# A hand-written order reworked: roots in two parts, decoding moved out of attention, eight first-layer units in a row, the last routing ahead of its weights

## The chip, the core and the metric

The kernel runs on one core of a Trainium2 chip. The metric is the device time of one execution in microseconds (us). The core has a matrix engine (TensorE, PE), a vector engine (VectorE, DVE), a scalar engine (ScalarE, ACT) and a general one (GpSimd, POOL), which take their instructions in the order of the program and wait for each other by semaphores; transfers are issued by SP's queue, and indirect ones (gather, scatter) by POOL.

## The reference

Three layers follow one another: attention with normalised queries and keys, a mixture with one expert (a leaky two-layer network whose weights come in 64-bit floats), and a mixture of eight experts in which each token goes to the one with the largest logit. Shapes: 4 batches, 12 heads, 448 rows, 64 columns a head; 1792 tokens of 768; 2048 columns in the first network, 1024 in each expert of the second.

```python
q_n, k_n = (rmsnorm(q, g_q), rmsnorm(k, g_k))        # x / sqrt(mean(x*x) + 1e-6) * g
scores = scale * np.matmul(q_n, k_n.transpose(0, 1, 3, 2))
scores = scores - np.max(scores, axis=-1, keepdims=True)
attn = np.exp(scores)
attn = attn / (np.sum(attn, axis=-1, keepdims=True) + 1e-09)
x = np.matmul(attn, v)                                # -> (1792, 768)

h = x @ w_in
x = np.maximum(0.01 * h, h) @ w_out                   # first MoE

logits = x @ w_gate
e_idx = np.argmax(logits, axis=1)
gate_w = probs[np.arange(N), e_idx]                   # softmax of the logits
eom = 1.0 / (1.0 + np.exp(-(x @ w_output_gate)))
for e in range(E):                                    # second MoE
    h = np.maximum(x[mask] @ w1[e], 0.0)
    out[mask] = gate_w[mask, None] * eom[mask, e, None] * (h @ w2[e])
```

## The kernel before

**Arithmetic.** Nearly every product is made of three matmuls: each operand is split into a high part (a copy on ACT) and a low part (the difference, `lo_of`, line 62, on DVE or POOL), and high by high, high by low and low by high are added in PSUM.

**Attention** works on 24 pairs of heads, two heads at a time on 128 partitions. Of each pair: `square`, `roots` and `norm` (DVE, POOL) normalise; `turn_q`/`turn_k` transpose; `top` makes the scores of one chunk of 112 rows and takes their row maxima into `md` (DVE); `row` transposes the four `md` on PE and copies them into `mx` (ACT, L296), which `probs` needs; `values` multiplies by V, and adds the probabilities into `pr` on POOL; `sums`, `spread`, `scale` and `store` divide by the sums and write the columns. While pair i has its `probs`, the tops of i+1 and the normalising of later pairs run beside it. A hand-written list says which step goes into which of the four quarters: `begin` (line 466) for pairs 0 to 2, `steady` for the others from `FROM` = 3, and `pieces` (line 380) for what stands ahead and behind.

**The first MoE** reads weights as pairs of 32-bit words. `Weights.half` (line 616) decodes half a tile in five steps, `magnitude`, `sign`, `flush`, `power` and `join`, with one DVE instruction each and, beside them, one on ACT and, at the end, an addition on POOL; `split` (line 651) makes the high half on ACT and the low half on POOL. There are 64 halves. Six of them (and one that starts them) are decoded within attention, at the pairs in `DECODE`. A unit m1 (`FirstMoe.first`, line 667) is one of 16 columns blocks f for one batch b: 18 matmuls into a `mo` bank (there are two), then `out`: g on ACT, the maximum on DVE, `gh` on ACT, `gl` on DVE. A unit m2 (`second`, line 690) is one of six output blocks d: 6 matmuls into an `mp` bank, of two f, added into `ysum`. Two f are a group G; there are eight groups, and a tile is a group for one batch. In group 0 the units are set in order by hand; from group 1 on each tile does the new m1 units, then the m2 units of the tile before, and `tile` (line 957) says which unit is followed by which steps of two halves.

**Routing** (`Route`, line 716) runs per batch: `logits` of six blocks, `read_logits` (`lt`), `turn_logits`, `pick` (the expert), `rank` and `place` (the slot of each token), `table` (matmuls of `A`, `Bm` that put token numbers and weights into `tab` and `stab`). `column` writes a block of the first MoE's output, turned, to `x2d` in DRAM through buffers `xn`. The last route runs behind the last m2 units. From `tab` follows `idx`, the list of tokens for each of 18 slot tiles.

**The second MoE** takes slot tile after slot tile: `gather` (POOL, indirect), `prep` (transposes, and `xgh`, `xgl`), `m1` into `ph`, `relu`, `turn`, `m2` into `py`, and a scatter. Expert weights come in the stretch before, as `w1h`, `w1l`, `w2h`, `w2l`. The order of PE, DVE, ACT and POOL is written by hand (`tc.manual_schedule`) up to the last route's choice, and again from the first gather.

## Time and profile before

| what | us |
| --- | --- |
| median of three runs | 1193.51 (1193.49, 1193.51, 1194.4) |
| the profiled execution | 1190.01 |
| its span in the trace | 1188.3 |
| PE busy in it | 1130.5 (95%) |
| mean granted clock | 0.981 |

The profile has one line an engine with its busy time, and lists of instructions with their start, their duration and, in brackets, how long the engine was idle before them and who ended that. PE being busy 95% says that it bounds the kernel, but this is a mean over stages: what can be won is read stage by stage, as idle time of PE and as stretches in which its clock is at the lower of its two levels.

### The profile page before, as it was taken

The page shows a single profiled execution, that of the slowest core. Times are in us where ns is not written, and L with a number is a line of the kernel's source. Part 1 is how long each engine was busy: PE and PEld are TensorE (multiplying, and loading weights), DVE is VectorE, ACT ScalarE, POOL GpSimd, SP SyncE. Part 2 cuts the span into 40 slices and gives each one's busy share as a digit, 9 for nine tenths or more (in the row PEclk, how much of TensorE's full clock was granted, in tenths as well). Part 3 has the DMA queues.
Part 4 walks back from the last instruction along what each step waited for, and adds up shares of the span by engine and source line. Part 5 has one row for each costly group of instructions (what it writes and reads, how often), then busy time and mean ns, then how long its engine had stood idle before and what let it go on. Part 6 is the DMA issues. An engine that isn't in the chain of part 4 may idle for free.

```text
span 1188.3 us, 18150 instructions
## 1 busy us (share of the span) xinstructions
PE 1130.5 (95%) x6620; PEld 912.5 (77%) x6620; DVE 809.8 (68%) x1384; ACT 496.4 (42%) x791; POOL 391.3 (33%) x267
## 2 busy tenths in 40 slices
PE   5899999998999999999999999998699999999997
PEld 3455555444689889998989898886599998998996
DVE  8787888988656888888888887354644179115445
ACT  4566666655444222222222222213443277225444
POOL 3767677777423322222222222000102113102022
PEclk9999999989999999999999999999699999999999
DMA  7222222111111211111111111523555169214446
GB/s 144 60 63 66 60 63 69 40 33 51 40 54 50 59 52 55 53 55 53 54 53 54 54 54 41 200 49 96 171 207 210 40 240 372 113 36 161 165 189 234
DMA packets 68075, 116.21 MB, mean 98 GB/s; under 512 B 6780, under 2 KB 45948, under 8 KB 67968
## 3 DMA queue, kind: packets, MB, share of 16 engines
q1 hardware_dynamic: 64848, 103.87, 27.5%
q0 software_dynamic: 3120, 11.02, 2.7%
q8 instruction: 54, 0.88, 0.3%
q14 instruction: 53, 0.43, 0.1%
HBM read 106.61 MB, written 12.58 MB: 100 GB/s over the span
## 4 chain that ended last, share of the span: by engine, by line
PE 76%; DVE 15%; issue 4%; ACT 4%; DMA 1%; POOL 0%; POOLq 0%; ACTq 0%; DVEq 0%
PE mp L697 6%; PE mp L699 6%; PE mp L698 6%; PE mo L674 5%; PE mo L675 5%; PE mo L676 5%; PE sc L310 5%; PE py L1158 4%; PE py L1156 4%; PE py L1157 4%; PE ph L1141 4%; PE av L321 4%; PE ph L1142 4%; PE ph L1140 4%; DVE md L289 3%
## 5 line engine op out<-in xcount | busy, mean ns | idle before, releaser
L326 POOL TENSOR_TENSOR pr<-pr,p 112x896 f32<-112x896 f32 x71 | 150.4, 2119 | 21.9 <-PE av L321 19.8
L645 POOL TENSOR_TENSOR raw<-raw,top 128x384 f32<-128x384 f32 x64 | 66.3, 1036 | 258.9 <-DVE raw L644 258.9
L697 PE MATMUL mp<-gh,w1h 128*128 128x448 f32 x384 | 144.2, 376 | 5.0 <-DVE ysum L705 2.5
L699 PE MATMUL mp<-gh,w1l 128*128 128x448 f32 x384 | 142.1, 370 | 1.2 <-POOL w1l L63 1.2
L674 PE MATMUL mo<-xTh,w0h 128*128 128x448 f32 x384 | 141.5, 369 | 1.0 <-DVE gl L63 1.0
L698 PE MATMUL mp<-gl,w1h 128*128 128x448 f32 x384 | 141.9, 370 | 0.2 <-DVE gl L63 0.2
L675 PE MATMUL mo<-xTl,w0h 128*128 128x448 f32 x384 | 140.8, 367 | 0.0
L676 PE MATMUL mo<-xTh,w0l 128*128 128x448 f32 x384 | 140.0, 365 | 0.0
L1204 POOL DMA_INDIRECT out_dram<-y,idx x18 | 36.1, 2004 | 264.1 <-DVEq L1199 149.6
L705 DVE TENSOR_TENSOR ysum<-mp,ysum 128x448 f32<-128x448 f32 x168 | 100.9, 616 | 18.7 <-PE mp L699 18.7
L289 DVE TENSOR_REDUCE md<-tp 112x2 f32<-112x896 f32 x94 | 101.9, 1084 | 15.7 <-PE tp L287 15.3
L63 DVE TENSOR_TENSOR hL<-pt,hT 128x512 fp32r<-128x512 f32 x36 | 24.9, 692 | 114.1 <-ACTq L1166 59.4
L1156 PE MATMUL py<-w2h,hT 128*128 128x384 f32 x288 | 99.8, 346 | 0.0
L1158 PE MATMUL py<-w2l,hT 128*128 128x384 f32 x288 | 96.8, 336 | 0.0
L1157 PE MATMUL py<-w2h,hL 128*128 128x384 f32 x288 | 96.6, 335 | 0.0
L682 ACT ACTIVATE g<-mo 128x448 f32<-128x448 f32 x64 | 34.8, 544 | 135.3 <-PE mo L676 135.3
L312 ACT ACTIVATE p<-sc 112x896 f32<-112x896 f32 x72 | 65.7, 912 | 55.5 <-PE sc L310 52.6
L1140 PE MATMUL ph<-w1h,xgh 128*128 128x512 f32 x216 | 86.1, 398 | 0.0
L1142 PE MATMUL ph<-w1l,xgh 128*128 128x512 f32 x216 | 85.1, 394 | 0.0
L1141 PE MATMUL ph<-w1h,xgl 128*128 128x512 f32 x216 | 85.1, 394 | 0.0
L697 PEld LDWEIGHTS mp<-gh,w1h 128*128 128x128 f32 x384 | 72.6, 189 | 14.9 <-DVE ysum L705 5.2
L699 PEld LDWEIGHTS mp<-gh,w1l 128*128 128x128 f32 x384 | 72.9, 190 | 8.4 <-POOL w1l L63 1.6
(207 smaller groups left out, 2444.8 us busy)
## 6 DMA issues: line engine op xcount, KB each, us to landing
r<-in_moe_w_dram SPq DMA_DIRECT2D x27, 1024.0 KB, 5.3
r<-in_moe_w_dram SPq DMA_DIRECT2D x36, 768.0 KB, 7.8
wd<-in_moe_w_in_dram SPq DMA_DIRECT2D x32, 384.0 KB, 3.4
wd<-in_moe_w_out_dram SPq DMA_DIRECT2D x32, 384.0 KB, 3.1
qk<-in_q_dram SPq DMA_DIRECT2D x24, 224.0 KB, 3.0
qk<-in_k_dram SPq DMA_DIRECT2D x24, 224.0 KB, 3.3
vv<-in_v_dram SPq DMA_DIRECT2D x24, 224.0 KB, 2.6
x2d<-xn SPq DMA_DIRECT2D x24, 224.0 KB, 3.0
```

Of the source, the lines that this page charges most:

```text
L289: nc.vector.tensor_reduce(st["md"][:, c, ::DH], sc[:CP, :, :S], AX.X, ALU.max)
L326: nc.gpsimd.tensor_tensor(st["pr"][:CP], st["pr"][:CP], p, ALU.add)
L674: nc.tensor.matmul(ph, wh_[:, c], xh, start=(c == 0), stop=False)
L675: nc.tensor.matmul(ph, wh_[:, c], xl, start=False, stop=False)
L676: nc.tensor.matmul(ph, wl_[:, c], xh, start=False, stop=(c == KD - 1))
L697: nc.tensor.matmul(py, hi[:, sl], gh, start=(j == 0), stop=False)
L698: nc.tensor.matmul(py, hi[:, sl], gl, start=False, stop=False)
L699: nc.tensor.matmul(py, lo[:, sl], gh, start=False, stop=(j == GF - 1))
L1140: nc.tensor.matmul(ph[n], xh[:, c], w1h[:, c, s_], start=(c == 0), stop=False)
L1156: nc.tensor.matmul(py[n], hT[:, c], w2h[:, c, s_], start=(c == 0), stop=False)
L1157: nc.tensor.matmul(py[n], hL[:, c], w2h[:, c, s_], start=False, stop=False)
L1158: nc.tensor.matmul(py[n], hT[:, c], w2l[:, c, s_], start=False, stop=(c == K2 - 1))
```

## The change

1. **Start.** `roots` can be done in two parts, of four and five instructions. `begin` has a new list: the pairs' roots from pair 1 on are done in the two parts a and b, `row` and `spread` stand behind `values`, `store` behind the turns. The first pair's four tops stand in a row, and `route_constants` comes ahead of the loop instead of in pair 12.
2. **Decoding.** `DECODE` has 21 and 22 only (it had 15, 17, 19, 20, 21, 22), so that four halves fewer are decoded within attention. The first `split` moves from the first to the last quarter of pair 22, and the one in the last section leaves it; the two fills are block f = 0 for batches 0 and 1. The order of weights goes by group: both input blocks, both output blocks.
3. **Group 0.** Eight m1 units stand in a row, with the halves h3 to h7 and their splits between them, then 24 m2 units with eight halves. The steady tiles get one step of decoding behind every six matmuls.
4. **Routing.** A table's matmuls stand a slot behind the `A`, `Bm` that they need, `Bm` is made on POOL, columns go in pairs. In the last route all six logit groups come first, the logits are read ahead of the columns, `xn` has buffers of its own, and no `w1l` stands in between. The weights (`weigh`, `stab`, `rsc`) move into slot tile 0, between the last `ph` and the first `py`. The first gather stands alone; `w1l` 1, 3, 5 are on DVE, and 0, 2, 4 on POOL behind that gather.

```diff
-        def roots(self, sts):
+        def roots(self, sts, parts=(0, 1)):
...
-            todo = ({0: ["s2"], 1: ["g2", "n2"], 2: ["q3"], 3: ["s3"]},
-                    {0: ["q4"], 1: ["s4"], 2: ["g3", "n3"], 3: ["q5"]},
-                    {0: ["s5", "q6"], 1: ["s6"], 2: ["g5", "q7"], 3: []})[i]
+            todo = ({0: ["s2"], 1: ["g2", "n2"], 2: ["q3"], 3: ["q4", "s3"]},
+                    {0: ["s4"], 1: ["a3"], 2: ["b3", "q5"], 3: ["q6", "s5"]},
+                    {0: ["s6"], 1: ["a5"], 2: ["b5", "q7"], 3: []})[i]
+            after = ({}, {2: (3,)}, {0: (4,), 2: (5,)})[i]
...
                     else:
-                        self.norm(sts[k], (1, 0))
-                if c == 3:
-                    self.row(one)
-                    if prev:
-                        self.spread(prev)
+                        self.roots(sts[k:k + 2], ("ab".index(op[0]),))
                 if c:
                     self.values(cur, c - 1)
...
                 elif c == 3:
+                    self.row(one)
                     if prev:
+                        self.spread(prev)
                         self.scale(prev)
...
-    DECODE = 15, 17, 19, 20, 21, 22
+    DECODE = 21, 22
...
-            self.order = [(kind, f) for kind in range(2) for f in range(GF)]
-            self.order += [(kind, f) for f in range(GF, NF) for kind in range(2)]
+            self.order = [(kind, f) for G in range(NG) for kind in range(2) for f in range(G * GF, (G + 1) * GF)]
...
-        if i == B * NPAIR - 2 and q == 0:
+        if i == B * NPAIR - 2 and q == 3:
             wts.split()
...
+    h4, h5, h6, h7 = (wts.half() for _ in range(4))
+    plan = [[wts.split, *h4[:1]], h4[1:3], h4[3:], h5[:2], h5[2:3], h5[3:], [wts.split, *h6[:1]]]
+    plan += [[x] for x in h6[1:4]] + [[h6[4], h7[0]], h7[1:2], h7[2:3], h7[3:], [wts.split]]
+    done = len(plan)
+    do([("m1", 0, 0, 2), ("m1", 0, 0, 3)] + [("m1", 0, 1, b) for b in range(B)], plan)
...
+            plan = [[x] for x in halves(0, 1)]
+            if b in (1, 3):
+                at(plan, 11, wts.split)
...
-    for d, unit in enumerate(group("m2", NG - 1, B - 1)):
-        steps = list(extra[d])
-        if d:
-            steps += [lambda d=d: late.logits(d - 1), lambda d=d: late.column(d - 1)]
-        moe.run(unit, steps)
-    late.logits(KD - 1)
-    late.column(KD - 1)
+    own = wts.pools[0]
+    for d in range(KD):
+        late.logits(d)
+    late.read_logits()
+    late.columns((0, 1), own)
+    late.turn_logits()
+    late.pick()
...
+        if t == 0:
+            weights_made()
         for c in range(4):
             m2(0, c)
...
+    def low1(c):
+        lo_of(nc.vector if c % 2 else nc.gpsimd, w1l[:, c], r1[c // 2][:, c % 2], w1h[:, c])
+
+    def weights_made():
+        n = NC * P
+        room = sb.tile([P, D], F32, name="y2")
+        late.weigh()
+        late.weigh_more()
+        pt = p2.tile([P, 3, P], F32, name="pt")[:, 0]
+        for c in range(NC):
+            Bm, A = room[:CP, c * P:(c + 1) * P], room[:CP, n + c % 2 * NTAB:n + (c % 2 + 1) * NTAB]
+            nc.gpsimd.tensor_scalar(Bm, place, late.pf[:, c:c + 1], None, ALU.is_equal)
+            nc.vector.tensor_scalar(
+                A, iota[:CP, :NTAB], late.col[:, c:c + 1], late.z[:, c:c + 1], ALU.is_equal, ALU.mult)
+            nc.tensor.matmul(pt[:NTAB], A, Bm, start=(c == 0), stop=(c == NC - 1))
+        nc.vector.tensor_tensor(stab, pt[:NTAB], stab, ALU.add)
+        pt = p2.tile([P, 3, P], F32, name="pt")[:, 0, :NSLOT]
+        nc.tensor.matmul(pt, stab, perm, start=True, stop=True)
+        nc.vector.tensor_copy(rsc, pt)
```

The first place is POOL's queue in the last section of attention, with the kernel before; `raw` is the addition that ends a half, `w0l` a split's low part, `pr` the sums of probabilities.

```order
L645 TENSOR_TENSOR raw<-raw,top 128x384
L326 TENSOR_TENSOR pr_126<-pr_126,p 112x896 x2
L63 TENSOR_TENSOR w0l<-raw,w0h 128x768
L326 TENSOR_TENSOR pr_124<-pr_124,p 112x896
L645 TENSOR_TENSOR raw<-raw,top 128x384
L326 TENSOR_TENSOR pr_124<-pr_124,p 112x896 x2
L63 TENSOR_TENSOR w0l<-raw,w0h 128x768
```

The same stretch of POOL after the change (its line numbers are those of the changed kernel).

```order
L645 TENSOR_TENSOR raw<-raw,top 128x384
L330 TENSOR_TENSOR pr_126<-pr_126,p 112x896 x2
L330 TENSOR_TENSOR pr_124<-pr_124,p 112x896
L645 TENSOR_TENSOR raw<-raw,top 128x384
L330 TENSOR_TENSOR pr_124<-pr_124,p 112x896
L63 TENSOR_TENSOR w0l<-raw,w0h 128x768
L330 TENSOR_TENSOR pr_124<-pr_124,p 112x896
L330 TENSOR_TENSOR pr_126<-pr_126,p 112x896 x2
```

The first `w0l` now stands behind a further `raw` and two more additions into `pr`.

The second place is DVE in group 0, with the kernel before; L683 is the maximum of a unit m1, `gl` its low part, L631 to L644 are the five steps of a half.

```order
L683 TENSOR_TENSOR mo<-mo,g 128x448
L63 TENSOR_TENSOR gl<-mo,gh 128x448
L683 TENSOR_TENSOR mo<-mo,g 128x448
L63 TENSOR_TENSOR gl<-mo,gh 128x448
L631 TENSOR_SCALAR top<-wd 128x384
L634 SCALAR_TENSOR_TENSOR top<-wd,top 128x384
L637 SCALAR_TENSOR_TENSOR top<-raw,top 128x384
L641 TENSOR_SCALAR raw<-top 128x384
L644 SCALAR_TENSOR_TENSOR raw<-wd,raw 128x384
L683 TENSOR_TENSOR mo<-mo,g 128x448
```

DVE in the eight units after the change.

```order
L685 TENSOR_TENSOR mo<-mo,g 128x448
L63 TENSOR_TENSOR gl<-mo,gh 128x448
L629 TENSOR_SCALAR top<-wd 128x384
L632 SCALAR_TENSOR_TENSOR top<-wd,top 128x384
L636 SCALAR_TENSOR_TENSOR top<-raw,top 128x384
L640 TENSOR_SCALAR raw<-top 128x384
L644 SCALAR_TENSOR_TENSOR raw<-wd,raw 128x384
L685 TENSOR_TENSOR mo<-mo,g 128x448
L63 TENSOR_TENSOR gl<-mo,gh 128x448
```

There is now a whole half between one unit and the next, in unit after unit.

The third place is DVE around slot tile 0, with the kernel before; `xgl` is the low part of the gathered rows, `w1l` and `w2l` those of the expert's weights, `hL` that of the hidden layer.

```order
L63 TENSOR_TENSOR xgl_8255<-pt,xgh_8253 128x384 x2
L63 TENSOR_TENSOR w1l<-r_1_7303,w1h 128x1024
L63 TENSOR_TENSOR w1l<-r_2_7304,w1h 128x1024 x2
L63 TENSOR_TENSOR w2l<-r_0_7305,w2h 128x768 x2
L63 TENSOR_TENSOR w2l<-r_1_7306,w2h 128x768 x2
L1125 TENSOR_LOAD flags
L63 TENSOR_TENSOR hL<-pt,hT 128x512
L63 TENSOR_TENSOR w2l<-r_2_7307,w2h 128x768 x2
L63 TENSOR_TENSOR w2l<-r_3_8244,w2h 128x768 x2
L63 TENSOR_TENSOR hL<-pt,hT 128x512
```

DVE there after the change, up to the first of the `w2l`.

```order
L63 TENSOR_TENSOR w1l<-r_0_7310,w1h 128x1024
L63 TENSOR_TENSOR w1l<-r_1_7311,w1h 128x1024
L63 TENSOR_TENSOR w1l<-r_2_7312,w1h 128x1024
L63 TENSOR_TENSOR xgl_8231<-pt,xgh_8229 128x384 x2
L63 TENSOR_TENSOR w2l<-r_0_7313,w2h 128x768 x2
```

And DVE from the first `hL` on; `kz`, `ksm`, L1253, `stab` and `rsc` make the weights.

```order
L63 TENSOR_TENSOR hL<-pt,hT 128x512
L63 TENSOR_TENSOR w2l<-r_2_7315,w2h 128x768 x2
L63 TENSOR_TENSOR w2l<-r_3_8220,w2h 128x768 x2
L835 TENSOR_REDUCE kz<-kz_8196 112x4
L841 TENSOR_REDUCE ksm<-kd_8195 112x4
L842 TENSOR_SCALAR ksm<-ksm 112x4
L843 TENSOR_SCALAR kz<-kz 112x4
L844 TENSOR_TENSOR kz<-kz,ksm 112x4
L845 RECIPROCAL kz<-kz 112x4
L1253 TENSOR_SCALAR y_8371<-iota,kcol,kz 112x112 x4
L1256 TENSOR_TENSOR stab<-pt,stab 112x128
L1259 COPY rsc<-pt 128x21
```

All `w1l` of DVE now stand ahead of `xgl`, and the weights' steps behind the four `w2l`.

## Rows read from the trace of the kernel before

**Rows 1.** Page, engines: busy us (share of the span) x instructions.

```profile
PE 1130.5 (95%) x6620; PEld 912.5 (77%) x6620; DVE 809.8 (68%) x1384; ACT 496.4 (42%) x791; POOL 391.3 (33%) x267
```

**Rows 2.** Windows: A:B us, busy (x instructions), PEclk, DMA share, GB/s.

```profile
73.72:162.63 88.91, 88.91 (x707) 47.58 (x708) 72.79 (x125) 60.04 (x89) 66.42 (x41) 1.00 0.22 63
162.63:276.43 113.80, 105.83 (x795) 54.76 (x796) 100.08 (x171) 67.62 (x102) 80.82 (x49) 0.97 0.17 48
315.80:388.00 72.20, 70.10 (x336) 63.53 (x333) 42.25 (x67) 31.89 (x60) 18.46 (x14) 0.98 0.17 51
388.00:745.00 357.00, 353.65 (x1717) 321.71 (x1718) 292.41 (x481) 94.79 (x170) 96.89 (x74) 1.00 0.18 53
745.00:827.65 82.65, 77.46 (x584) 67.24 (x586) 41.52 (x140) 18.76 (x40) 1.40 (x1) 0.98 0.38 117
827.65:852.46 24.81, 14.62 (x92) 11.40 (x92) 11.72 (x51) 9.68 (x15) 3.21 (x3) 0.62 0.35 94
```

**Rows 3.** Windows, stretches at the lower clock level.

```profile
58.88:62.29 3.41, 3.24 (x12) 1.50 (x12) 1.47 (x3) 1.89 (x5) 3.29 (x3) 0.50 0.45 135
260.26:267.09 6.83, 6.83 (x26) 2.95 (x25) 3.82 (x10) 3.17 (x6) 4.33 (x3) 0.50 0.20 58
331.94:335.36 3.42, 3.33 (x9) 2.99 (x10) 2.90 (x8) 1.30 (x3) 0.03 (x1) 0.50 0.00 0
813.22:816.64 3.42, 3.42 (x14) 3.13 (x13) 2.82 (x11) 0.00 (x0) 0.00 (x0) 0.50 0.02 5
833.70:854.18 20.48, 13.21 (x59) 10.26 (x60) 12.71 (x51) 8.99 (x14) 4.21 (x4) 0.50 0.31 88
```

**Rows 4.** Waits of PE, 0 to 90: total us, times, longest us.

```profile
PE tr L294 <- DVE md L289: 6.3, 4, 3.7
```

**Rows 5.** Timeline, DVE and POOL: start us, us, instruction.

```profile
53.37 2.06 DVE L220 TENSOR_SCALAR y<-ms 112x32 int32<-112x32 int32 x1
...
51.12 4.28 POOL L326 TENSOR_TENSOR pr<-pr,p 112x896 f32<-112x896 f32 x2
```

**Rows 6.** Timeline, POOL's second `w0l`, and PE's first use of one.

```profile
305.49 1.83 POOL L63 TENSOR_TENSOR w0l<-raw,w0h 128x768 fp32r<-128x768 f32 x1
...
304.45 0.36 PE L676 MATMUL mo<-xTh,w0l 128*128 128x448 f32 x1
```

**Rows 7.** Windows, a half decoded alone, and one beside POOL.

```profile
349.88:352.42 2.54, 2.54 (x14) 2.32 (x14) 2.33 (x7) 1.34 (x4) 0.00 (x0) 1.00 0.17 68
364.53:368.63 4.10, 4.10 (x21) 3.76 (x21) 3.89 (x7) 2.83 (x7) 1.85 (x1) 1.00 0.17 59
```

**Rows 8.** Groups of DVE, 388 to 745: busy us, mean ns, idle.

```profile
L63 DVE TENSOR_TENSOR gl<-mo,gh 128x448 fp32r<-128x448 f32 x49 | 30.6, 624 | 29.9 <-ACT gh L684 29.9
L683 DVE TENSOR_TENSOR mo<-mo,g 128x448 f32<-128x448 f32 x48 | 30.0, 626 | 20.9 <-ACT g L682 20.9
```

**Rows 9.** Waits of PE, 745 to 827.65.

```profile
PE mp L697 <- ACT gh L684: 1.8, 1, 1.8
```

**Rows 10.** Timeline, last route to first `ph`: ACT, DVE, POOL, PE.

```profile
834.16 0.26 ACT L748 ACTIVATE lt<-lg 128x112 f32<-128x112 f32 x1
...
835.53 1.22 DVE L63 TENSOR_TENSOR w1l<-r,w1h 128x1024 fp32r<-128x1024 f32 x1
...
846.62 1.21 POOL L1108 DMA_INDIRECT xg<-x2d,idx  x1 [100.22 <-DVE idx L1069]
...
852.46 0.80 PE L1140 MATMUL ph<-w1h,xgh 128*128 128x512 f32 x1
```

**Rows 11.** Timeline, a decoding step of DVE and a POOL split.

```profile
324.36 2.11 DVE L634 SCALAR_TENSOR_TENSOR top<-wd,top 128x384 int32<-128x384 int32 x1
...
324.21 1.84 POOL L63 TENSOR_TENSOR w1l<-raw,w1h 128x768 fp32r<-128x768 f32 x1 [9.65 <-ACT w1h L657]
```

**Rows 12.** Timeline, slot tile 0: DVE, PE.

```profile
860.99 3.55 DVE L63 TENSOR_TENSOR w2l<-r,w2h 128x768 fp32r<-128x768 f32 x4
...
862.14 0.33 PE L1156 MATMUL py<-w2h,hT 128*128 128x384 f32 x1
```

More of the change, by code (lines that the diff above doesn't have):

```diff
@@ L602, in fetch @@
             kind, f = self.order[k]
-            own = self.more if g and self.more else dec
+            own = self.more if self.more and not g else dec
             wd = own.tile([P, n, 2], I32, name="wd", bufs=WD)
@@ L953, in do, with halves @@
     def do(units, plan=()):
-        for u, unit in enumerate(units):
-            moe.run(unit, plan[u] if u < len(plan) else ())
-    def tile(first, second, end):
-        a, b_ = wts.half(), wts.half()
-        return [first + a[:3], a[3:] + b_[:2], [], b_[2:3], b_[3:4], b_[4:], end]
+        slots = [list(x) for x in plan]
+        for unit in units:
+            moe.run(unit, slots)
+        for step in sum(slots, []):
+            step()
+    def halves(*ks):
+        return sum((wts.half() for _ in ks), [])
@@ L961, in attention_moe_moe2, with at @@
+    def at(plan, slot, *steps):
+        while len(plan) <= slot:
+            plan.append([])
+        plan[slot] += steps
+        return plan
+    wts.fetch()
     outs[0]()
-    while fills:
-        fills.pop(0)()
+    h3 = wts.half()
+    moe.slots(fills, [h3[:2], h3[2:4]])
+    for step in h3[4:]:
+        step()
     outs[1]()
-    wts.split()
-    half = wts.half()
-    do(group("m1", 0, 1), [half, [wts.split]])
     nc.vector.tensor_scalar(place, iota[:CP], HALF, 1.0 / P, ALU.subtract, ALU.mult)
-    half = wts.half()
@@ L983, in attention_moe_moe2 @@
+    plan = [ops[len(ops) * i // slots:len(ops) * (i + 1) // slots] for i in range(slots)]
+    do(group("m2", 0, 0) + group("m2", 0, 1), plan[:slots // 2])
+    sM.close()
+    my1 = sE.enter_context(tc.tile_pool(name="my1", bufs=1, side="right"))
+    y.append(my1.tile([P, B // 2, KD, S], F32, name="y1"))
+    do(group("m2", 0, 2) + group("m2", 0, 3), plan[slots // 2:])
     sG.close()
     moe.mw = sE.enter_context(tc.tile_pool(name="mwh", bufs=1, side="right"))
-    plan = tile([wts.split], [], [])
@@ new lines, in attention_moe_moe2 @@
+        if wts.halves < 2 * len(wts.order):
+            plan = [[x] for x in halves(0, 1)]
+            if b in (1, 3):
+                at(plan, 11, wts.split)
+        if b == 1 and G > 1:
+            plan = at(plan, 0) and [[wts.split] + plan[0]] + plan[1:]
+        if b == 3:
+            plan[3] = [wts.split] + plan[3]
+        if (G, b) == (NG - 1, 2):
+            route = Route(0, (pp, 1), rt)
+            plan = route.steps()
+            for k, pair in enumerate(route.pairs()):
+                plan[k] = pair + plan[k]
@@ L1031, in attention_moe_moe2 @@
                 ld()
-    late = Route(B - 1, (pc, 2), rt)
-    extra = [s2[4:5], s2[5:6] + c2[1:2], s2[6:7] + c2[2:3], s2[7:9], s2[9:11], s2[11:]]
-    for d, unit in enumerate(group("m2", NG - 1, B - 1)):
-        steps = list(extra[d])
-        if d:
-            steps += [lambda d=d: late.logits(d - 1), lambda d=d: late.column(d - 1)]
-        moe.run(unit, steps)
-    late.logits(KD - 1)
-    late.column(KD - 1)
-    for step in c2[3:]:
+    one, two = Route(1, (pp, 1), rt), Route(2, (pp, 1), rt)
+    s1, s2 = one.steps(), two.steps()
+    plan = s1[:6]
+    for k, pair in enumerate(one.pairs()):
+        plan[k] = pair + plan[k]
+    do(group("m2", NG - 1, B - 2), plan)
+    plan = s1[6:]
+    for k, (pair, step) in enumerate(zip(two.pairs() + [[], []], s2)):
+        plan[k + 1] = plan[k + 1] + step + pair
+    first, last = group("m1", NG - 1, B - 1)
+    moe.run(first, plan)
+    chunks, put = moe.first(last[2], last[3])
+    while chunks:
+        for step in chunks[:GF]:
+            step()
+        chunks = chunks[GF:]
+        if not chunks:
+            put()
+        for step in plan.pop(0):
+            step()
+    pB.close()
+    pc = pB.enter_context(tc.tile_pool(name="pc", bufs=2, space=bass.MemoryType.PSUM, side="right"))
+    late = Route(B - 1, (pc, 2), rt, kept=True)
+    late.count()
+    do(group("m2", NG - 1, B - 1), s2[5:11])
+    own = wts.pools[0]
[5 more added lines that the diff above has]
+    late.pick()
+    for step in s2[11]:
         step()
-    late.choose()
-    ordered.close()
+    late.columns((2, 3), own)
+    late.rank(last=True)
+    late.columns((4, 5), own)
+    late.place(last=True)
     def mm_small(lhsT, rhs, m, n):
```

322 lines of the change are left out of this document (148 added, 174 removed).

## The prediction

> **What bounds the kernel now.** I read the engine line of the page first [rows 1]: TensorE (PE) is busy for 1130.5 of 1188.3 us, and no other engine comes near. So time can be won in two places only: where PE is idle, 57.8 us in all, and where its granted clock is down. The second view is therefore the table of windows, one line for each stage [rows 2]. In the eight attention pairs from 73.72 to 162.63 PE is busy for all of 88.91 us, 11.11 a pair. In the nine pairs after them the same work takes 113.80. The first MoE from 388 to 745 has 3.35 idle, the routing stretch up to 827.65 has 5.19, and the 24.81 us from the last `mp` matmul to the first matmul of the second MoE are 10.19 idle at a clock of 0.62. The third view gives the stretches at the lower of the two clock levels, 0.50 [rows 3]: two of 3.41 us near the start (one is shown), 6.83 in the pairs, 3.42 in the first MoE, 3.42 in the routing, 20.48 around its end. In each but the last PE was nearly always busy, so work that takes 3.41 would have taken 1.7. I read them as what follows where PE has stood still. The change touches all of these places and adds no matmul of size, so I sum place by place, on the profiled execution of 1190.0 us.
>
> **Start, 0 to 73.7: -4 (-1 to -7).** PE's row transpose of `md` waits 6.3 us for the maxima, four times, 3.7 at the longest [rows 4], and about 3.4 go to the low clock. What holds the maxima back is the chain of nine `roots` instructions in front of the last of them, one of which took 2.06, beginning while two POOL additions of 4.28 ran and ending with them [rows 5], where its neighbours take 0.2. The change puts five of the nine behind the last maximum and matmuls (`values`, `sums`) ahead of the row. It can't give more than 6.3 + 3.4 = 9.7. The long instruction stays ahead of the maxima and can meet POOL again, so I take half, -4.8. Against it stand `route_constants`, now at the very start, and a Q turn that goes behind the first row: +0.8: the three shorter of the four waits are (6.3 - 3.7)/3 = 0.9 each, and I take one more of that size.
>
> **Pairs 12 to 20: -13.8 (-11 to -14).** Nine pairs at 11.11 are 100.0; they took 113.8 [rows 2]. The four decoded halves that leave (pairs 15, 17, 19, 20) and the route constants of pair 12 are all that tells these pairs from the eight before, apart from the low-clock stretch in them [rows 3], which began as PE fell behind. With the DVE and POOL work gone the pairs are the eight again, so I take all of it. The lower end allows that the first fetches of weights, now in the last pairs, or POOL's additions still cost 3. The two halves decoded in pairs 21 and 22 stay as they are and cost what they cost.
>
> **The first split: +1.9 (+1 to +3).** In the last section the POOL queue now has a further half and two more `pr` additions ahead of `w0l`, and ACT makes `w0h` only after the last `xTh`. The third matmul of the first fill needs `w0l`; it ran at 304.45 [rows 6] with no wait, the low half being there long before. A split made there ends 1.83 after it begins on POOL [rows 6], and nothing is late beside it: +1.9.
>
> **Eight first-layer units in a row: +0.3 (-3 to +5).** Gone are 2.1 idle between 315.80 and 388.00 [rows 2], 1.7 of low clock, and some 1.9 of the idle after 388 where group 0 ends: -5.7. New is a bound by DVE. A unit has 18 matmuls; 336 took 70.10 there [rows 2], so 3.76. A half decoded undisturbed takes DVE 2.54, one beside a POOL split 4.10 [rows 7]; the unit's own `mo` and `gl` take 0.626 and 0.624, with 29.9/49 = 0.61 of waiting for ACT between them [rows 8]. One half per unit makes 2.54 + 1.86 = 4.40, which is 0.64 more than PE needs. With two `mo` banks PE can't run ahead: five such units lose 3.2, and a lock by one split adds up to 1.56, which gives about 5, and 1 for a dip of the clock behind it. The upper end has 4.10 for most halves. The 24 `m2` units that follow have 30.1 us of PE for eight halves, which is cover enough.
>
> **The other groups: -0.5 (-2 to +1).** 24 tiles took 357.00, 14.9 each, DVE busy for 12.2 of it [rows 2]. The new order sets one step of decoding behind each six matmuls. The 3.35 idle can only shrink a little.
>
> **Routing, 745 to 827.65: -5.8 (-3 to -7).** Of 5.19 idle 1.8 is one wait for `gh` [rows 9], which I leave, since a unit still follows its own activation; of the other 3.4, mostly waits for the route's `A`, `oh` and logits, which now stand a slot apart, I take 3.2 off. A low-clock stretch is worth 1.7 [rows 3], which may or may not go: I take 0.3 us off for it. Logits and two columns of the last route leave this stretch for the next: -2.3, paid for in the next term.
>
> **The last route: -7.5 (-6 to -8.5).** From the end of the last `mp` at 827.65 to the first gather at 846.62 are 18.97 us [rows 10]. The logits were read only at 834.16, behind `xn` copies that waited for buffers, and two `w1l` of 1.22 stood in the choice of the expert [rows 10]. In the new order the logits of all six chunks come first, an estimated 2.0, then the read at about 829.7; from there the old chain of 846.62 - 834.16 = 12.46 runs without 2.4 of `w1l` and without a part of the waits for the weights' `A`. The gather begins 11.2 to 12 after the last `mp`. From gather to first `ph` matmul (846.62 to 852.46) I leave 5.84.
>
> **Low halves on two engines: +4.5 (0 to +6.4).** `w1l` 0, 2, 4 now stand on POOL behind the first gather, 1, 3, 5 on DVE, and DVE's `xgl`, which the second `ph` matmul needs, stands behind all three. A `w1l` takes DVE 1.22 [rows 10]. On POOL I estimate 1.83 x 1024/768 = 2.44 [rows 6]. If the two run side by side, DVE's three are done in 3.7, before the gathered rows land, and the cost is 0. The trace shows what a DVE instruction with two inputs in SBUF does beside a POOL one: `L634` took 2.11 and ended with POOL's `w1l`, which had begun 0.15 earlier and took 1.84 [rows 11]; alone it is one of five that take 2.54 together. If they alternate, one POOL and one DVE piece take 3.66, and `xgl` is ready 9.2 to 10.4 after the gather instead of 5.8. `w1l` too has two inputs in SBUF, so I take that row: +4.5.
> The Trainium skill, page "SBUF — State Buffer", section "Who interferes with whom", states a rule that speaks against this part: a DVE `tensor_tensor` with both inputs in SBUF contends with GpSimd reads, by an exclusive lock. By it the term would be +4.5, without it 0. The trace agrees for the scalar forms, as in rows 11; no run yet shows it for this form.
>
> **Weights in slot 0: +6.2 (+4 to +7), and +1.5 for the clock.** Before, the first `py` matmul began at 862.14 [rows 12], straight after the last `ph`. Now four `A`/`Bm` matmuls and the `perm` matmul stand between the two on PE. On DVE their six small steps and four `A` stand behind four `w2l` which before ended at 860.99 + 3.55 = 864.54 [rows 12]. Six steps (1.3), four `A` (4 x 0.33, the last overlapped), the sum into `stab` and the copy behind it bring the first `py` to about 868.3: 6.2 later. PE stands still for it, and the longest halt at the start, 3.7 [rows 4], was followed by a low-clock stretch of 3.41, worth 1.7 [rows 3]: +1.5, between 0 and 3.4.
>
> **The sum.** -4 - 13.8 + 1.9 + 0.3 - 0.5 - 5.8 - 7.5 + 4.5 + 6.2 + 1.5 = -17.2, so a profiled execution of 1172.8. The median before, 1193.5, stands 3.5 above its profiled execution; on that scale I forecast 1176.3.
>
> **Rivals.**
> A, the sum as it stands: 1176.3, chance 0.60.
> B, the tail's new waits do not bite: the two engines run side by side and DVE gets to the weights earlier. For it: POOL has little else to do there. Against it: rows 11 and the order of DVE's queue. It takes off 4.5 and about 3 of the 7.7: 1168.8, chance 0.19.
> C, the eight units are bound by DVE at 4.10 a half: 6 units at 4.10 + 1.86 - 3.76 = 2.2 each lose 13 instead of 5: 1184.3. Against it: only one half in two to three meets a split. Chance 0.13.
> D, the other side, slower than before: in the steady groups each decoding step now stands alone between PE's slots and can meet POOL's additions and splits more often. DVE has 14.9 - 12.2 = 2.7 idle a tile, of which 1.2 are the fixed waits for ACT of two units [rows 2, 8]; 1.5 a tile is left, for two halves. A half may lengthen by 0.7 before anything shows, and the kernel loses its 17 when each lengthens by (17.2/24 + 1.5)/2 = 1.1. The worst pair of rows says 4.10 - 2.54 = 1.56: 24 x (3.1 - 1.5) = +39, so about 1215. Against it: DVE's load per tile is the same, and the halves already meet POOL in many cases. Chance 0.04.
> E, the decoding was not what slowed pairs 12 to 20; the excess stays, less the route constants: -1 instead of -13.8: 1189.1. Against it: the eight pairs without decoding have no idle at all. Chance 0.04.
>
> **How the numbers follow.** The terms' ends, taken as independent, give about 8 either way around A. The range has to take in B (1168.8) and most of C; leaving out the outer parts of B, C, D and E as the two in ten, it is 1166 to 1187. A measurement of this kernel tells 0.2% (2.4 us) from no change. Slower by more than that is D alone, with part of its chance: 0.03. Within it are the milder D, and an E with one more term gone: 0.04. Faster: 0.93.
>
> **What would show it.** In the changed kernel's trace the row copies `mx` should come every 11.11 us up to pair 20; the first fill's third matmul should wait about 2 for `w0l`; the eight units should show `mo` waiting for DVE by some 5 in all; the first gather should begin 11 to 12 after the last `mp`; the second `ph` matmul should wait for `xgl`, with DVE's and POOL's `w1l` in turns; and `py` should wait some 6 in slot 0. I am wrong if the pairs still take over 12 us without decoding, if PE's idle in the steady groups grows beyond 10 us, or if the tail after the last `mp` shrinks by more than 5 us in spite of the two new waits.

## The result, and the profile after

The changed kernel takes 1180.68 us (median of four runs, 1179.36 to 1182.49) against 1193.52 before: a ratio of 0.9892, 95% interval 0.9875 to 0.9909, so 12.8 us faster. Forecast was 1176.3, between 1166 and 1187. The profiled execution took 1180.47, at its kernel's median; that of before, 1190.01, was 3.5 below its own. So the two traces are 9.5 us apart where the medians are 12.8 apart, and the terms below are read against 9.5, not 12.8.

The first view is the table of windows of the changed kernel: the pairs 4 to 20 (counted from 0, as in the code; in [rows 2] they are the first two lines, 8 and 9 pairs), from the second m1 unit to group 1's first `mp`, the other groups, the routing, the last `mp` to the first `ph`, and slot tile 0. From the second line on the borders lie near those of [rows 2], not at the same matmuls; the table below compares the same matmuls (its routing ends at the start of the last `mp`, 0.2 before the window's).

```profile
69.80:258.71 188.91, 188.91 (x1499) 101.16 (x1499) 153.73 (x267) 125.67 (x186) 140.09 (x86) 1.00 0.17 52
302.21:379.20 76.99, 73.26 (x344) 65.00 (x343) 59.05 (x95) 35.54 (x69) 26.41 (x21) 0.98 0.24 72
379.20:732.70 353.50, 353.50 (x1729) 324.56 (x1728) 271.41 (x475) 92.94 (x166) 95.80 (x72) 1.00 0.18 52
732.70:806.22 73.52, 68.28 (x510) 61.52 (x509) 35.93 (x123) 16.96 (x37) 7.12 (x12) 0.95 0.42 132
806.22:824.23 18.01, 11.85 (x122) 9.53 (x121) 11.43 (x32) 9.79 (x14) 9.37 (x8) 0.71 0.47 137
824.23:859.15 34.92, 25.33 (x109) 21.80 (x109) 19.12 (x29) 10.41 (x18) 12.04 (x11) 0.76 0.56 215
```

In the first and the third line PE's busy time is the whole line: the 17 pairs have no idle left, and neither have the tiles of the other groups. The last line is the new weak spot: 9.6 us idle and a clock of 0.76 in one slot tile.

Measured between the starts of the same instructions in both traces, stage by stage:

| stage | forecast | measured (before, after) |
| --- | --- | --- |
| start, to the fifth `mx` | -4 | -3.9 (73.72, 69.80) |
| pairs 12 to 20 | -13.8 | -13.8 (202.71, 188.91 for pairs 4 to 20) |
| pairs 21, 22 | 0 | -0.7 (24.76, 24.09) |
| first split and last section | +1.9 | +2.9 (16.52, 19.41) |
| group 0 | +0.3 | +2.1 (74.90, 76.99) |
| other groups | -0.5 | -4.9 (358.40, 353.51) |
| routing | -5.8 | -3.0 (76.29, 73.32) |
| last route, to the first `ph` | -7.5 | -7.0 (25.17, 18.21) |
| slot tile 0 (both new waits, clock) | +12.2 | +15.8 (19.16, 34.92) |
| 17 further slot tiles | 0 | +2.5 (308.66, 311.15) |
| sum | -17.2 | -10.0 |

The two spans differ by 9.6; the 0.4 left over lie behind the last matmul.

The second view is PE's waits over the whole span that the terms speak of (us in total, times, longest). Left out above them are 8.8 at the very start (8.9 before), 4.5 for the row maxima and 4.3 for the first gathered rows. Before, the start's row transpose stood at 6.3 in the first 90 us [rows 4]; in the whole span it is 0.8 now.

```profile
...
PE ph L1166 <- DVE xgl L63: 5.5, 1, 5.5
...
PE ch L862 <- POOL Bm L853: 3.7, 1, 3.7
PE pt L1255 <- DVE y L1253: 3.6, 1, 3.6
PE mo L675 <- DVE gl L63: 2.0, 2, 1.8
...
PE mp L699 <- ACT y L705: 1.2, 2, 1.0
PE mo L677 <- POOL w0l L63: 1.2, 1, 1.2
PE tr L260 <- ACT mx L300: 1.0, 3, 0.4
PE tr L298 <- DVE md L293: 0.8, 3, 0.4
```

The first four lines shown are the price of the change: `xgl` and the weights (`y` is the room in which `A` and `Bm` of the weights are made) in slot tile 0, as forecast; `Bm`, which was not; and the `mo` wait of the eight units. The third view gives the stretches at the lower clock level, five here and six before (five of them in [rows 3]); one of 5.1 at the very end, in both, is left out.

```profile
288.26:291.67 3.41, 3.41 (x28) 1.65 (x26) 0.75 (x3) 0.92 (x2) 1.43 (x1) 0.50 0.00 0
315.56:318.98 3.42, 3.42 (x11) 3.03 (x10) 2.63 (x6) 0.76 (x2) 1.00 (x1) 0.50 0.19 43
755.88:762.71 6.83, 6.06 (x19) 5.47 (x20) 3.31 (x9) 0.87 (x3) 2.45 (x4) 0.50 0.00 1
813.91:834.39 20.48, 9.58 (x30) 6.94 (x31) 17.63 (x24) 9.70 (x12) 17.59 (x15) 0.50 0.54 183
844.63:851.46 6.83, 6.20 (x21) 5.62 (x22) 1.40 (x5) 0.00 (x0) 0.00 (x0) 0.50 0.47 177
```

Those at the start and in the pairs are gone in this execution. The one at 813.91 was there before (833.70). Each of the other four begins at one of the new waits or right behind it: 288.26 (`w0l`), 315.56 (`mo`), 755.88 (`Bm`), 844.63 (the weights).

### The profile page after: what moved, and what is told of

It is laid out like the page before. It is cut to its first block, busy times and chain, and to the rows that moved or that the text cites. A ratio compares the mean times of both kernels' runs of the same rounds, so it can differ in the third digit from the quotient of the medians.

```text
span 1178.7 us, 18179 instructions
## 1 busy us (share of the span) xinstructions
PE 1125.7 (96%) x6620; PEld 914.1 (78%) x6620; DVE 787.8 (67%) x1362; ACT 494.6 (42%) x791; POOL 412.9 (35%) x293
## 4 chain that ended last, share of the span: by engine, by line
PE 85%; DVE 8%; ACT 3%; issue 2%; DMA 1%; POOL 1%; SPq 0%; ACTq 0%; POOLq 0%; DVEq 0%
PE sc L314 7%; PE mp L699 6%; PE mp L701 6%; PE mp L700 6%; PE av L325 6%; PE mo L675 6%; PE mo L677 6%; PE mo L676 6%; PE py L1181 4%; PE py L1183 4%; PE py L1182 4%; PE ph L1166 4%; PE ph L1167 4%; PE ph L1165 4%; PE tr L260 2%
## 5 line engine op out<-in xcount | busy, mean ns | idle before, releaser
L707 DVE TENSOR_TENSOR y<-mp,y 128x448 f32<-128x448 f32 x168 | 101.0, 616 | 18.2 <-PE mp L701 18.2
L675 PEld LDWEIGHTS mo<-xTh,w0h 128*128 128x128 f32 x384 | 72.5, 189 | 12.0 <-DVE gl L63 3.6
```

The costliest lines, as they stand in the source:

```text
L675: nc.tensor.matmul(ph, wh_[:, c], xh, start=(c == 0), stop=False)
```

## The experiments

All times are medians of the kernel named; what a stage gave is read between the same instructions in its trace and in that of the changed kernel, because the start alone differs by up to 4 us from execution to execution (the fifth `mx` came between 68.3 and 72.2 in the twelve traces with the changed start, those of the result and of all runs but the one with the old start).

### The two engines on `w1l`

The order of the changed kernel's low halves, DVE, POOL and PE around the first `ph`. The first line is DVE's first `w1l` by itself.

```profile
819.17 8.55 DVE L63 TENSOR_TENSOR w1l<-r,w1h 128x1024 fp32r<-128x1024 f32 x1 [0.20 <-ACT w1h L1239]
...
818.38 1.24 POOL L1133 DMA_INDIRECT xg<-x2d,idx  x1 [2.26 <-DVE fl L1103]
819.66 6.97 POOL L63 TENSOR_TENSOR w1l<-r,w1h 128x1024 fp32r<-128x1024 f32 x3
...
830.51 0.80 PE L1166 MATMUL ph<-w1h,xgl 128*128 128x512 f32 x1 [5.49 <-DVE xgl L63]
```

One `w1l` of DVE takes 8.55 us and ends at 827.72, 1.1 after the last of POOL's three; POOL's three follow each other without a gap. DVE's other two stand behind it, and `xgl` with them. In all nine traces with this order the first `w1l` took 8.3 to 8.6 us and ended 1.1 after POOL's third.

First run, all `w1l` on DVE:

```diff
-        lo_of(nc.vector if c % 2 else nc.gpsimd, w1l[:, c], r1[c // 2][:, c % 2], w1h[:, c])
+        lo_of(nc.vector, w1l[:, c], r1[c // 2][:, c % 2], w1h[:, c])
...
     for c in range(K1):
+        if c == LW:
+            for g in range(2):
+                prep(0, g)
         low1(c)
-    for g in range(2):
-        prep(0, g)
```

> The changed kernel with all six `w1l` on DVE again, three ahead of `xgl` and three behind it, as in the kernel before; nothing of them on POOL. Theory (the two engines shut each other out): the three `w1l` ahead of `xgl` take 3.7 instead of 10.82, the second `ph` matmul waits 0 instead of 5.5 us, and the time is 1180.7 - 5.5 = 1175.2, down to 1173.5 if the low-clock stretch there gets shorter too. Rival (what is won is given back at the weights' wait in slot 0, since DVE has three more `w1l` to do): the `xgl` wait goes, the wait for `py` grows by 3 to 4, and the time is 1178 to 1179.

Measured: 1175.16, ratio to before 0.9842 (0.9824 to 0.9860). DVE's three ahead of `xgl`:

```profile
820.43 3.47 DVE L63 TENSOR_TENSOR w1l<-r,w1h 128x1024 fp32r<-128x1024 f32 x3
825.84 1.20 DVE L63 TENSOR_TENSOR xgl<-pt,xgh 128x384 fp32r<-128x384 f32 x2 [1.94 <-ACT xgh L1143]
```

They take 3.47 instead of 10.82, `xgl` is not waited for, and slot tile 0 is 29.56 instead of 34.92 long: -5.4. The weights' wait is 3.7 where it was 3.6, so nothing is given back there. The theory holds, the rival falls.

Second run, the split kept, `xgl` first:

```diff
+    for g in range(2):
+        prep(0, g)
     for c in range(K1):
         low1(c)
-    for g in range(2):
-        prep(0, g)
```

> The changed kernel with DVE's `xgl` ahead of its three `w1l`; POOL still makes `w1l` 0, 2, 4. Theory (DVE's `w1l` can't run while POOL's do): `xgl` isn't waited for, DVE's first `w1l` ends only after POOL's three are done, some 7 us after the first gather's issue, and PE waits 2 to 3 us for a `w1l` instead of 5.5 for `xgl`: 1177 to 1178.5. Rival (only the place in DVE's queue was wrong, nothing is shut out): DVE's first `w1l` ends 1.2 after `xgl`, PE waits under 1, and the time is 1175 to 1176.

Measured: 1177.91, ratio 0.9876 (0.9859 to 0.9892). DVE and POOL there:

```profile
823.90 2.48 DVE L63 TENSOR_TENSOR w1l<-r,w1h 128x1024 fp32r<-128x1024 f32 x1
...
820.60 4.69 POOL L63 TENSOR_TENSOR w1l<-r,w1h 128x1024 fp32r<-128x1024 f32 x2
```

POOL ends at 825.29, DVE's `w1l` 1.1 later: held again, though only POOL's third was still to run, for 1.4 us. `xgl`, with one input in PSUM, ran beside POOL at its own pace, 1.20 for both. DVE's `w1l` ended 2.4 after `xgl`, not 1.2 as the rival has it. But PE then waits only 1.0 for a `w1l`, not 2 to 3, and slot tile 0 is 30.03 long, -4.9. So the theory has the mechanism and the median, and its price was too high: DVE is held by POOL, and what that costs is set by what stands behind the `w1l` in DVE's queue.

### The weights in slot tile 0

```diff
         relu(1)
-        if t == 0:
-            weights_made()
...
         for c in range(4, K2):
             m2(0, c)
+        if t == 0:
+            weights_made()
         for c in range(4, K2):
             m2(1, c)
```

> The changed kernel with the weights of the last route made later in slot tile 0: behind the `py` matmuls of the first output half, ahead of the last four chunks. Theory (the first `py` waits for the weights' chain on DVE, nothing else): the first `py` follows the last `ph` at once, the PE waits of 3.6 and 0.4 go, and with them the 6.8 us at the low clock behind them, worth 3.4: 1180.7 - 4 to 1180.7 - 7.4, so 1173.3 to 1176.7. Rival (the chain is late wherever it stands, since DVE's `w2l` and the scatter need it): the wait moves to the new place and the time stays within 1.5.

Measured: 1176.54, ratio 0.9866 (0.9849 to 0.9884). The same PE wait in this trace:

```profile
PE pt L1255 <- DVE y L1253: 1.1, 2, 0.9
```

The first `py` follows the last `ph` at once. Of 3.6 us 1.1 are left, the 0.4 behind them stay, the low-clock stretch is 3.41 instead of 6.83, and slot tile 0 is 3.9 shorter. The theory holds, with the smallest gain that it allowed.

### The routing that lost half of its gain

The wait for `Bm` at 756.65 was not in the prediction. Back along the chain in the changed kernel, ACT, DVE, POOL, PE:

```profile
750.89 1.84 ACT L755 ACTIVATE xn<-mt 112x512 f32<-112x512 f32 x3 [4.64 <-DMA x2d<-xn]
...
753.20 0.63 DVE L685 TENSOR_TENSOR mo<-mo,g 128x448 f32<-128x448 f32 x1 [3.73 <-ACT g L684]
...
755.88 2.45 POOL L853 TENSOR_SCALAR Bm<-place,pf 112x128 f32<-112x128 f32 x4 [28.20 <-DVE pf L827]
...
756.65 1.35 PE L862 MATMUL ch<-Bm,A 112*112 112x128 f32 x4 [3.73 <-POOL Bm L853]
```

Six columns in three slots in a row want six `xn` buffers, and there are three; so ACT stands for 4.64 behind the transfer of the first, the `g` of the m1 unit behind ACT's copy, DVE's maximum behind `g`, the token's place behind that, and the table on PE at the end. PE names POOL, which was only the last link.

```diff
             for k, pair in enumerate(route.pairs()):
-                plan[k] = pair + plan[k]
+                plan[4 * k] = pair + plan[4 * k]
```

> The changed kernel with route 0's three pairs of columns in slots 0, 4 and 8 instead of 0, 1 and 2. Theory (ACT stands behind a column's copy that waits for one of three buffers, and `g`, `mo`, the place and the table wait behind it): ACT's wait of 4.6 for the DMA goes, PE's wait of 3.7 for `Bm` and the 6.8 us at the low clock behind it go: 1180.7 - 7.1 = 1173.6. Rival (`Bm` is late because POOL makes it, four in 2.45 us): PE still waits 2.5 or more for `Bm`, and the time is 1179 to 1180.7.

Measured: 1176.14, ratio 0.9855 (0.9838 to 0.9871). ACT's wait for the transfers in the routing, from 730 to 800, in the changed kernel and in this one:

```profile
ACT xn L755 <- DMA x2d<-xn: 5.3, 2, 4.6
```

```profile
ACT xn L755 <- DMA x2d<-xn: 1.3, 2, 0.7
```

PE does not wait for `Bm` any more, and the routing takes 68.12 instead of 73.32, -5.2. The 6.83 us at the low clock are gone from there; a stretch of 3.41 appears at 794.3, which is why it is 5.2 and not 7.1. The theory holds, the rival falls: POOL still makes `Bm`, and PE does not wait for it.

### Decoding put back into the pairs

The first half is decoded again in four pairs, all steps, then without POOL's addition. In `half`, with the fetch moved ahead to pair 14:

```diff
-                if g == 0:
+                if g == 0 and len(self.raw) == k:
...
-                wd = self.wd.pop(h)
+                wd = self.wd[h] if again else self.wd.pop(h)
...
                 nc.gpsimd.tensor_tensor(dst, dst, at["top"].bitcast(F32), ALU.add)
+                if again:
+                    return
...
-        if i in DECODE:
+        if i in DECODE or i in AGAIN:
...
-                work.half = wts.half()
+                work.half = wts.half(i in AGAIN)
...
+    AGAIN = 15, 17, 19, 20
```

> The changed kernel in which pairs 15, 17, 19 and 20 decode the first half again (the same values, into the same tile), all five steps with POOL's addition. Its real decoding stays in pairs 21 and 22. Theory (decoding is what slows the pairs): pairs 12 to 20 take 11.11 each up to 14 and lose 12 to 13 in all from 15 on: 1180.7 + 12.8 = 1193.5. Rival (the route constants or the low clock slowed them, not the decoding): the pairs stay at 11.11 and the time within 1.5 of 1180.7.

Measured: 1193.67, ratio 1.0000 (0.9982 to 1.0017); its ten executions spread from 1190.7 to 1197.6, and the profiled one took 1196.43.

In the second kernel the early return stands ahead of the addition:

```diff
+                if again:
+                    return
                 nc.gpsimd.tensor_tensor(dst, dst, at["top"].bitcast(F32), ALU.add)
-                if again:
-                    return
```

> As the run with repeated decoding, but the repeats leave out POOL's addition; ACT's and DVE's steps stay. If DVE is what is short in these pairs (its maxima come late), it loses most of the same, 9 to 13: 1190 to 1193.5. If POOL's queue is (the additions into `pr` and the normalising stand behind the half's addition), it loses under 4: 1181 to 1184.5.

Measured: 1191.35, ratio 0.9980 (0.9971 to 0.9990). Two pairs, the one that decodes and the next, with POOL's addition (first fence) and without (second):

```profile
194.26:207.28 13.02, 11.55 (x91) 5.95 (x91) 12.16 (x16) 7.94 (x13) 8.99 (x5) 1.00 0.19 55
207.28:219.34 12.06, 11.39 (x91) 5.96 (x92) 11.05 (x22) 7.51 (x13) 9.78 (x7) 1.00 0.06 20
```

```profile
192.41:205.44 13.03, 11.57 (x91) 5.96 (x92) 12.17 (x16) 7.95 (x13) 11.15 (x6) 1.00 0.19 55
205.44:216.56 11.12, 11.12 (x91) 5.95 (x91) 10.03 (x22) 7.51 (x12) 6.70 (x5) 1.00 0.08 22
```

The decoding pair has DVE busy for 12.16 us, more than the 11.11 that PE needs, and takes 13.0: 1.9 lost to the steps of DVE and ACT, which no run separates. POOL's addition costs another 0.95, in the pair after it. Pairs 4 to 20 took 203.94 with all steps and 197.96 without POOL's, against 188.91: 15.0 and 9.1. Of the 15.0 some 2.1 are not decoding alone: pair 18 took 14.20 where the kernel before has 12.06, with a stretch of 6.83 us at the low clock from 232.31 that was not there before; the other pairs from 15 on agree with the kernel before within 0.03. The remaining 12.9 stand against 13.8 before, and the route constants of pair 12 (12.08 before, 11.1 now) are the difference. So decoding is the cause of what the pairs lost, and the part of DVE and ACT is the larger. Both forecasts hold in the medians.

### The start, and the first split

```diff
-            todo = ({0: ["s2"], 1: ["g2", "n2"], 2: ["q3"], 3: ["q4", "s3"]},
-                    {0: ["s4"], 1: ["a3"], 2: ["b3", "q5"], 3: ["q6", "s5"]},
-                    {0: ["s6"], 1: ["a5"], 2: ["b5", "q7"], 3: []})[i]
+            todo = ({0: ["s2"], 1: ["g2", "n2"], 2: ["q3"], 3: ["s3"]},
+                    {0: ["q4"], 1: ["s4"], 2: ["g3", "n3"], 3: ["q5"]},
+                    {0: ["s5", "q6"], 1: ["s6"], 2: ["g5", "q7"], 3: []})[i]
...
+                if c == 3:
+                    self.row(one)
+                    if prev:
+                        self.spread(prev)
                 if c:
                     self.values(cur, c - 1)
...
```

> The changed kernel with the start of the kernel before: `roots` in one piece, the old list of `begin` and the old opening; the route constants stay ahead of the loop. Theory (roots in parts and the row behind the values gave the start's gain): the fifth `mx` comes 3.9 later, near 73.7, and the time is 1184.6; with the route constants there too up to 1185.5. Rival (the start's gain lies elsewhere, or is taken back as the pairs run into the same DVE limit): within 1.5 of 1180.7.

Measured: 1184.15, ratio 0.9915 (0.9899 to 0.9932). PE's waits from 0 to 90 in this kernel:

```profile
PE tr L298 <- DVE md L293: 7.1, 4, 4.4
```

The fifth `mx` comes at 74.53 instead of 69.80. The theory holds: +3.5 in the medians, +4.7 in the traces, and the wait of before is back (7.1; [rows 4] has 6.3). Which part of the new start gives how much (the roots in parts, the row behind the values, the four tops in a row) is not separated.

```diff
-    DECODE = 21, 22
+    DECODE = 20, 21
...
-        if i == B * NPAIR - 2 and q == 3:
+        if i == B * NPAIR - 2 and q == 0:
             wts.split()
```

> The changed kernel with its two halves decoded in pairs 20 and 21 instead of 21 and 22, and the first split at the first quarter of pair 22 instead of the last. Theory (the first fill waits for `w0l`, split too late): the wait of 1.2 and the low-clock stretch of 3.4 behind it go, 2.9 in all, while the decoding costs in pair 20 what it cost in 22: 1177.8. Rival (the fills are late for another reason, ACT's `xTh` or POOL's additions): within 1 of 1180.7.

Measured: 1179.82, ratio 0.9882 (0.9865 to 0.9898). From the last `mx` to the second m1 unit 16.21 us instead of 19.41: the first split's price is 3.2, as the theory says. But pair 20 with decoding takes 14.38 and pair 21 13.82, where the changed kernel's pairs 21 and 22 take 12.28 and 11.81; pairs 4 to 22 lose 3.3, and nothing is left. The time lies within the rival's 1 us of 1180.7, but not for the rival's reason: the fill's price is what the theory says, and the expectation was wrong in taking a half to cost the same in pair 20 as in 22.

### What adds up, and the place of the buffers

The three edits of slot tile 0 and the routing together:

> The changed kernel with three of the edits together: all `w1l` on DVE around `xgl`, the weights later in slot 0, route 0's columns in slots 0, 4 and 8. By the three runs' traces these gave 5.4 (first `ph` to second slot), 3.9 (the same stretch) and 5.2 us (routing). Theory (three separate places): they add up, 14.5, to 1166.2. Rival (they share the slack of DVE in slot 0, or the clock's dips behind the waits are counted twice): the stretch of slot 0 gives 6 to 7 instead of 9.3, and the time is 1168.5 to 1169.5.

Measured: 1163.80, ratio 0.9762 (0.9741 to 0.9783). Slot tile 0 takes 23.64, 11.3 less, more than the 9.3 of the two apart, since no low-clock stretch begins in it any more; the routing 68.28. The places are separate, and the time lies 2.4 below the sum that was expected.

In every kernel with the change a slot tile took 18.31 us, before 18.17, with the same work. `w1h` and `w1l` lie 928 bytes a partition higher than before, and so do the six buffers that stand ahead of them on the same side and take the weights as they are loaded (`r1`, `r2`). Two kernels leave room ahead of all eight, 96 bytes as shown, or 32:

```diff
             wr = ctx.enter_context(tc.tile_pool(name="wr", bufs=1, side="left"))
+            wr.tile([P, 24], F32, name="pad")
```

> The changed kernel with 96 bytes a partition left free ahead of the expert weights' buffers, so that `w1h` and `w1l` begin at 66528 and 91104 instead of 66432 and 91008; nothing else is moved. In every run of the changed kernel's kind a slot tile takes 18.31 us, and 18.17 before, where `w1h` begins at 65504. Theory (the place of `w1h` and `w1l` in SBUF sets the pace of the `ph` matmuls; 66528 and 65504 are alike modulo 512): slots of 18.17, 2.4 us less in 17 slots. Rival (something else, the code or the transfers beside them): 18.31 stays.

> As the run with 96 bytes, but 32 bytes are left free: `w1h` begins at 66464, like the kernel before modulo 64 but not modulo 512. If the place matters modulo 64, slots take 18.17; if only modulo 512, or not at all, 18.31.

Sixteen slot tiles (from the second to the last) in the kernel before, the changed one, with 96 bytes, and with 32, each from its own trace:

```profile
871.62:1162.29 290.67, 290.67 (x1570) 264.84 (x1570) 135.06 (x168) 133.48 (x201) 50.66 (x32) 1.00 0.46 165
```

```profile
859.15:1152.16 293.01, 293.01 (x1569) 264.88 (x1569) 135.01 (x168) 133.55 (x201) 51.33 (x32) 1.00 0.45 162
```

```profile
859.67:1150.34 290.67, 290.67 (x1570) 264.83 (x1569) 135.01 (x168) 133.49 (x201) 50.59 (x32) 1.00 0.45 163
```

```profile
861.50:1154.30 292.80, 292.80 (x1570) 264.93 (x1569) 135.02 (x168) 133.60 (x201) 51.32 (x32) 1.00 0.45 162
```

With 96 bytes the sixteen take 290.67 again, to the hundredth; with 32 only 0.2 of the 2.3 us comes back. The times, of one execution each, are 1178.44 and 1182.66; the slots are the measure here. It sits in the `ph` matmuls alone, whose first of three goes from 403 ns in the changed kernel to 396 with 96 bytes (the other two from 395 to 392 and from 397 to 393):

```profile
L1165 PE MATMUL ph<-w1h,xgh 128*128 128x512 f32 x192 | 77.4, 403 | 0.0
```

```profile
L1166 PE MATMUL ph<-w1h,xgh 128*128 128x512 f32 x193 | 76.4, 396 | 0.0
```

The place of the buffers is the cause: `w1h` at 65504 and 66528, alike modulo 512, is fast, at 66432 and 66464 slow, and the last is like the first two modulo 64. That "nothing else is moved" is not so: `r1` and `r2` move by the same bytes, and no run moves them without `w1h` and `w1l`; the `ph` matmuls read only the latter two. Why the place matters, and whether 512 is the step, stays open with four places.

The last kernel has the three edits and the 96 bytes:

> The three edits together and the 96 bytes. If the buffers' place is what lengthens the slots: 2.4 below the run with the three edits, 1163.8; if not, the same as that run within 0.5.

Measured: 1160.70, ratio to before 0.9736 (0.9715 to 0.9757), 3.1 below the run with the three edits. Its slot tiles take 18.17 again, sixteen of them 290.67, which repeats the result of the 96 bytes. It is faster than both kernels: 20 us below the changed one, or 18.6 by the two ratios to the kernel before, whose median beside these last runs was 1.5 lower.

## Why the prediction was right, and where not

The time fell where it was forecast to, faster and within the range, 4.4 us above the point. Part of that nearness is luck: between the traces 7.7 us are missing (9.5 for 17.2), and in the table terms that came out worse, by 12.3 in all, stand against others that came out better, by 5.1. Step by step:

- **Pairs 12 to 20, last route** were right in mechanism and size (-13.8, -7.0 for -13.8, -7.5). The step "With the DVE and POOL work gone the pairs are the eight again" is what the runs with decoding put back show. The first gather begins 12.0 after the last `mp`, where 11.2 to 12 was forecast.
- **Start** has the size (-3.9 for -4) and half of the mechanism. The row's wait went from 6.3 to 0.4 in the first 90 us, but the tops now wait 4.1 for the maxima (first line before, second after), and 1.0 is a new wait for `mx`.

```profile
PE tp L287 <- DVE md L289: 1.4, 2, 1.0
```

```profile
PE tp L291 <- DVE md L293: 4.1, 4, 1.3
```

This execution had no stretch at the low clock there; four of the twelve with the changed start have 6.83 or 10.24 us of it, and their fifth `mx` comes at 70.7 to 72.2. The median of the twelve is 70.2, against 73.72 and 74.53 in the two traces with the old start; the run with the old start gives back 3.5 to 4.7. That half of the start's ceiling was taken happened to fit.

- **The first split** measured +2.9 for +1.9. "nothing is late beside it" failed: the wait itself is 1.2, but the clock falls behind it (288.26) for 3.41 us, worth 1.7, which the sum had in other places and not here.
- **Group 0** measured +2.1 for +0.3. What the matmuls lose can be added up from the distances between their starts, which are 0.205 us where nothing holds them. The old stalls, 5.2 in this stretch before, are gone, nearly the 5.7 of the forecast. New are 3.1 for the `mo` waits (2.0 of them shown as waits) and 1.6 for the clock, 4.7 where about 6 was forecast; and 1.8 for ACT's `y` copies and 0.6 for a `w1l`, which I had not costed: 7.1 in all.
- **The other groups** are the largest miss on the good side, -4.9 for -0.5. "The 3.35 idle can only shrink a little" failed: PE is now busy for 353.50 of 353.50 us. The wait that went is this one of the kernel before:

```profile
PE mp L697 <- DVE ysum L705: 2.5, 7, 0.9
```

It shows as 2.5 us of idle time, but at the same seven halts the starts of the matmuls lose 4.4: the record of the matmul ahead of a halt (0.37 long, where the next could start after 0.205) covers its beginning, and the first matmul behind it takes 0.30 to its successor's start. So the idle time that the forecast went by was too small a ceiling. DVE's work fell from 289 to 271 us between the same matmuls, with nearly as many instructions (478, 475); the five steps of a half take 3.13 us in the mean instead of 3.47, and its step `sign` 0.55 instead of 0.98. Rival D had the direction of this wrong. That setting one step behind each six matmuls does it is argued; no run takes that part out alone.

- **Routing** measured -3.0 for -5.8. The waits "which now stand a slot apart" did go (`A`, `oh` and the logits, 3.2 in all, are 0), but the term left out a resource that I did not count: three `xn` buffers for six columns in a row. It cost PE 3.7 and 6.83 us at the low clock; the run with the columns apart gives 5.2 back.
- **Slot tile 0** was the largest miss on the bad side, +15.8 for +12.2. Of the lock's term, 4.5 was forecast and 5.4 measured: right in kind, but "If they alternate" is not what happens; DVE gets no turn until POOL is through. [rows 11] already points there: `L634` did not end with POOL's `w1l`, as I read it, but 0.42 after it. The first `py` came 7.1 later for 6.2. The rest is the low clock, from 824 to 834 and 844 to 851, about 3 for the 1.5 of the sum; with both edits 11.3 of the 15.8 go away.
  The rule that I weighed, in the Trainium skill, page "SBUF — State Buffer", section "Who interferes with whom", is borne out for `tensor_tensor` by these runs: 8.55 us beside POOL, 1.2 without. That issue order decides who blocks, as that section of the Trainium skill also says, can't be read from the recorded starts: in nine traces DVE's instruction starts 0.2 to 0.6 us before POOL's first `w1l` and is held all the same. POOL's gather was on at that time, but it is not what held DVE: with all `w1l` on DVE the first began beside the gather too and took 1.20. Why DVE did not come first stays open.
- **The 17 further slots**, +2.5, were in no term: no part of the change touches them but by the place of the expert weights' buffers.
- **The scale.** The profiled executions are 9.5 apart, where 17.2 was forecast; the 3.5 by which the one before lay under its median had no counterpart after (0.2), and this hid 3.3 of the error.

Rivals B (no new waits) and E (decoding not the cause) fell by the runs above. C, the eight units bound by DVE at 4.10 a half, did not come either: two halves met a split of POOL (their step `sign` took 2.10 and 2.22 us, 0.56 alone), and PE stood for 1.8 behind one and 0.1 behind the other.

## What to carry to other kernels

Count the buffers, not only the order: putting copies in a row that wait for a transfer can stop an engine on whose next instruction a chain of others hangs, and the wait is then shown under the last link's name. Before splitting elementwise work with two SBUF inputs over DVE and POOL, see what stands behind it in DVE's queue: here DVE got nothing until POOL had finished its run. Idle time shown for a halt can be less than what the halt costs; the distance between the starts of the matmuls tells it. The largest gain came from moving elementwise work out of pairs in which DVE had more to do than PE, into tiles where it had room; and work that is needed late (the weights) belongs behind matmuls that can do without it.
